# Recurrent gated attention and a gated MLP on one core: the written-out order of 944 operations, kept up to entry 385 and rewritten, with its engines, from there on

## Chip, core and metric

The kernel runs on one core of a Trainium2 chip. The metric is the device time of one execution in microseconds (us), the median of several runs; lower is better.

## What is computed

A recurrent attention over 768 steps (4 batches, 8 heads of 48) feeds a gated MLP block. The reference, cut:

```python
for t in range(S):                                      # B, H, S, D = 4, 8, 768, 48
    state = alpha[:, :, t, :, None] * state + einsum('bhd,bhe->bhde', k[:, :, t], v[:, :, t])
    y[:, :, t] = einsum('bhd,bhde->bhe', q[:, :, t], state)
x = y.transpose(0, 2, 1, 3).reshape(B, S, H * D)        # [4, 768, 384]
h = maximum(x @ w_in, 0)                                # d_ff = 1024
u, v = h[..., :512], h[..., 512:]
v_n = (v - mean(v)) / sqrt(var(v) + 1e-6)
v_s = einsum('ts,bsd->btd', w_spatial, v_n) + b_spatial[None, :, None]
return (u * v_s) @ w_out                                # [4, 768, 384]
```

## The kernel before, in words

The sequence of each batch is cut into six chunks of 128 steps; chunk n is chunk n mod 6 of batch n // 6, so there are 24. Within a chunk the recurrence becomes matrix products: running sums of log alpha (`cums`, function `single`, line 870), their exponentials (`einvs`, `eexps`, `ebc`), scaled k and q (`kts`, `qts`), their transposes for two chunks at once (`trk`, function `two_singles`, line 974; the two copies out of PSUM are `evs`), the scores (`sc`) and their masking (`ms`), the state's update (`upd`, then `z`, `S`, `sb` in `carry`, line 382) and the output (`y`), whose copy out is `xe`. Chunks 10 to 23, with which the change has to do, all go through `single` and `two_singles`; the earlier ones go in pairs and fours.

The MLP follows per batch b: `v.b.tt` and its relu `ve`, statistics `bn`, `rs`, `nm` and normalization `vn` (`project_v`, line 1054); `u.b.ft.th` and its relu `ue` (`project_u`, line 1103); the product with w_spatial `s.b.d.th` in two parts, the bias `se` and the gate `g` (`mix`, line 1122); the output product `o.b.tt`, its copy `oe.n` (n = 6b + tt) and its store `st.n` (`project_out`, line 1159). The u, v, s and o products all go through one helper, so line 1005 stands for all of them in the profile; likewise 178, 180, 184, 186 and 189 are helper lines for copies, relus and multiplications on any engine.

Each operation is made once as an object with a number, the engines it may run on, its dependencies and the PSUM banks that it takes. Nothing decides their order at run time. The table `PLAN` (line 42) lists all 944 in order, and `replay` (line 109) emits them as listed: the letter is the engine (P TensorE, D VectorE, A ScalarE, G GpSimd, S the SyncE queue that issues DMAs), the number is the operation, and what follows @ is its PSUM bank. An engine works its entries strictly in the order of the table; an entry waits for its dependencies and, when it takes a bank, for all readers of what the bank held before. There are eight banks. All loads and stores are issued by the one queue S; the loads of chunks 8 to 23 (q, k, v, alpha: `qcs`, `kcs`, `vcs`, `acs`) are 192 KB each in rows of 192 bytes, into rings of three slots for two chunks each. The last four output tiles are staged in the buffer of the first four, so that copies `oe.20` to `oe.23` wait for the stores `st.0` to `st.3`.

Numbers that are used below:

| table number | operation |
|---|---|
| 498, 564 | `lns`, log of alpha, chunks 12 and 15 (on A) |
| 499, 511, 565 | `cums`, running sums, chunks 12, 13 and 15 (on P) |
| 413 | `upd`, update of the state, chunk 10 (on P) |
| 374, 378, 372 | `u.1.1.0`, `u.1.3.0`, `u.1.0.0` (on P); their relus are 375, 379, 373 |
| 369, 380 | `v.1.2`, `v.1.3` (on P); their relus are 370, 381 |
| 419, 424 | `y`, chunks 10 and 11 (on P); their copies are 420, 425 |
| 266, 269, 272 | `o.0.3`, `o.0.4`, `o.0.5` (on P) |
| 368, 385 | `vn.1.1`, `vn.1.2` |
| 742, 748 | `trk`, transposes of chunks 18 and 19; `sc.18`, the scores that need both its copies, 743 and 744; 797 is one of the copies of the next pair |
| 452 | `s.1.2.0.0`, the first `s` of batch 1 in the new order |
| 701, 747, 756, 795, 846 | copy `oe.12` and casts `sb.18`, `sb.19`, `vbs.21`, `vbs.22` |
| 671, 691, 915 | `g.2.0.0`, `g.2.1.1`, `g.3.1.1`, gates; 907, 911 are `g.3.3.0`, `g.3.0.1` |
| 850, 857, 863, 872 | chunk 23: load of v, its cast `vbs`, the state's `S` of chunk 22, `y.23` |
| 704, 705 | `oe.13` and its store; 493, 265 and 259 are the stores `st.11`, `st.2` and `st.0` |
| 942 | `oe.23.1`, the last copy out of PSUM |

Of the kernel before, what the change touches and what calls it, by code (L numbers as in the profile page):

```python
# [57 lines left out]
D255 P348@7,6 D243 D327 D350 A393 P344@4 A394 P338@5 G31 G328 D397 D330 D349 G396 P404@3 A345 A339 A405 A406 P257@1  # L58
A395 S495 S390 A258 P260@4 P359@2 S402 G407 G248 G326 G329 S494 S560 P346@0,7 D408 P354@3,5 P410@1,6 A360 D331 A347
A353 A411 D356 D355 P362@2 G252 G398 P351@7 A352 P357@3 D412 S508 S497 S509 P421@6,1 P416@5,0 D361 S496 S507 S562 S550  # L60
S548 S611 S561 S551 S549 A358 A363 D418 D423 P511@7 P369@3 P413@0 P374@2 P380@1 D414 D417 A261 A512 P378@0 D422 A498
D364 A375 A564 P263@5 P499@6 G244 G332 G409 G256 A370 A379 A513 D371 G415 A500 A501 P419@0 P424@3 A425 G517 G505 G503
D381 D382 D516 G515 A420 P266@2 P269@4 A502 A365 A383 A270 D366 D504 P429@0 P426@1 P438@3 P440@6 D384 A368 A430 A427
P436@4 A437 A441 A385 D264 D439 P272@0 D367 D267 D428 D431 D386 P521@1 P372@4 A514 A273 P565@6 P376@2 A377 A432 A552
P442@7 A568 P529@0 D443 D522 P456@3 D433 D434 A435 A566 A567 D373 P452@7 P553@1 P518@2,5 A519 A554 A556 D520 A555 P457
D458 D530 D570 G569 G523 G557 G459 P444@4 P445 P448@5 D446 P453 D454 P468@6 P449 D558 D450 P533@7,4 P524@2,0 P572@1,3
D525 G451 G455 P472@5 P469 P460@2 P473 D526 D534 D535 G531 G447 D474 S623 A559 P575@7 D576 A573 P461 S625 S612 S563
A615 D470 D462 P616@4 P527@5 P536@1 A627 S613 A574 P579@7,3 P588@6,0 G577 A617 A528 D589 A618 A537 P628@5 A629 A571
G475 P538@2 A630 P464@1 S624 S614 S730 S718 S721 S626 S720 G620 D621 D581 D580 S733 S732 P476@6 G631 G578 P541@3
P584@7 A539 A619 A542 P465 S784 S719 A477 D632 P634@5,4 D590 A636 D466 D585 S731 A722 P591@3 S786 S772 S785 S773 S835  # L70
S774 A592 S787 S775 G622 G532 P582@1 A583 D635 D540 P637@7 P482@6 A633 A483 P723@5 G586 G471 D638 G639 A724 P645@3,4
P640@0,2 D543 G463 G587 P479@7 P604@6 P596@1 D646 D642 D641 A734 A726 D647 G729 G467 A605 A741 G727 P593@3 P600@6 A594
P735@0 D606 D595 A738 D480 P648@4 P643@3 A544 D545 D546 D597 A649 P488@2 A644 A788 A601 A489 D547 P653@4 P660@7 P745@6
A654 D746 D655 A736 A607 D608 D610 P491@3 P664@4 A661 A665 A737 P650@6 A492 A776 G739 P598@1 D651 D609 P485@4 D652
# [1190 lines left out]
```

## Time and profile before

| | |
|---|---|
| median of 3 runs | 138.32 us (138.22 to 139.34) |
| span of the profiled execution, first to last instruction | 137.9 us |
| granted TensorE clock | 1.000 |
| loads and stores by SyncE's queue | 28.32 MB |

The profile is of one execution. A time in a timeline is the start in us from the span's start, followed by the duration; equal instructions in a row are merged, and then the duration runs to the end of the last. A bracket at a line's end is the idle time of the engine before it and what ended it. A window's row gives the length of the stretch, then each engine's busy time with its instructions in brackets, the granted clock, the share of the 16 DMA engines and GB/s. The border between the kept entries and the others lies at about 54 us on TensorE; S works entries of the kept part until 62.65 us.

### The profile page before, as it was taken

The numbers are of one execution on the slowest core, as the hardware profiler recorded it, in microseconds if no ns is written. First come the engines' busy times: TensorE is split into PE (matmuls) and PEld (weight loads), VectorE is DVE, ScalarE is ACT, GpSimd is POOL, SyncE is SP. The second block draws the span as 40 slices with busy tenths as digits, with TensorE's granted clock in tenths as the row PEclk, the third lists the DMA queues.
The fourth block names the chain that finished last, engine by engine and source line by source line (L and its number), as shares of the span: only waits on it lengthen the run. The fifth ranks groups of instructions, "written<-read, shape, count | busy, mean of one in ns | idle before, by whom it ended". The sixth has DMA issues, their size and how long they took to land.

```text
span 137.9 us, 5298 instructions
## 1 busy us (share of the span) xinstructions
PE 130.1 (94%) x2108; PEld 79.4 (58%) x2122; DVE 120.2 (87%) x300; ACT 107.7 (78%) x261; POOL 86.6 (63%) x146
## 2 busy tenths in 40 slices
PE   6999998999999999799999999999999999999990
PEld 3365555565566556466657676656576765566560
DVE  6259999989989999899899999997999999974960
ACT  3476998999999799699997989999865796953040
POOL 7355899993499799761079989520799841004550
PEclk9999999999999999999999999999999999999999
DMA  3999999499989788699999898999960597101064
GB/s 88 370 372 381 344 349 361 106 373 382 355 162 281 159 168 165 124 186 188 193 204 201 164 209 156 189 186 216 213 134 5 187 349 270 63 0 57 0 233 172
DMA packets 76521, 28.66 MB, mean 208 GB/s; under 512 B 63056, under 2 KB 74960, under 8 KB 76496
## 3 DMA queue, kind: packets, MB, share of 16 engines
q1 hardware_dynamic: 76464, 28.32, 77.8%
q8 instruction: 16, 0.26, 0.8%
q14 instruction: 9, 0.07, 0.2%
q0 software_dynamic: 32, 0.00, 0.0%
HBM read 23.60 MB, written 4.72 MB: 205 GB/s over the span
## 4 chain that ended last, share of the span: by engine, by line
PE 60%; DMA 19%; POOL 8%; issue 3%; SPq 3%; ACT 3%; DVE 0%; POOLq 0%; ACTq 0%
PE bank L1005 43%; DMA raw_w<-in_moe_w_spatial_dram 6%; DMA kc<-in_k_dram 5%; DMA raw_w<-in_moe_w_out_dram 4%; DMA ac<-in_alpha_dram 4%; PE bank L960 3%; SPq L883 3%; PE bank L944 2%; PE bank L988 2%; PE bank L416 2%; POOL w_row L180 2%; POOL kt L189 2%; PE bank L932 1%; PE bank L898 1%; POOL state L189 1%
## 5 line engine op out<-in xcount | busy, mean ns | idle before, releaser
L1005 PE MATMUL bank<-w_spT,vn 128*128 128x384 bf16 x192 | 35.6, 327 | 0.0
L189 POOL TENSOR_TENSOR gT<-vs,uT 128x384 bf16<-128x384 f32 x28 | 25.7, 933 | 14.1 <-DVE vs L1152 14.1
L189 POOL TENSOR_TENSOR kt<-kc,binv 128x384 bf16<-128x384 f32 x22 | 20.2, 928 | 22.3 <-ACT binv L908 15.2
L1005 PEld LDWEIGHTS <-vn 128*128 128x128 bf16 x192 | 17.5, 98 | 11.2 <-issue 0.3
L1005 PE MATMUL bank<-w_in,xT 128*128 128x512 bf16 x58 | 17.4, 380 | 1.6 <-ACT xT L178 0.7
L1005 PE MATMUL bank<-xT,w_in 128*128 128x384 bf16 x96 | 18.7, 326 | 0.0
L1005 PE MATMUL bank<-w_out_sb,gT 128*128 128x384 bf16 (+1 forms) x100 | 18.4, 320 | 0.0
L1152 DVE TENSOR_TENSOR vs<-bank,bsp_bc 128x384 f32<-128x384 f32 x31 | 16.3, 549 | 2.4 <-PE bank L1005 2.3
L949 DVE TENSOR_TENSOR ptm<-bank,mask 128x512 bf16<-128x512 f32 x28 | 17.9, 682 | 0.5 <-PE bank L944 0.3
L178 ACT COPY kqT<-bank 128x512 bf16<-128x512 bf16 (+1 forms) x20 | 15.0, 793 | 3.1 <-PE bank L988 1.9
L1067 DVE BATCH_NORM_STATS2 stats<-v_sb 128x6 f32<-128x512 bf16 x24 | 16.4, 683 | 0.6 <-ACT v_sb L184 0.5
L184 ACT ACTIVATE v_sb<-bank 128x512 bf16<-128x512 f32 x20 | 11.7, 597 | 2.0 <-PE bank L1005 1.7
L184 ACT ACTIVATE uT<-bank 128x384 bf16<-128x384 f32 x27 | 12.4, 494 | 0.7 <-PE bank L1005 0.6
L1005 PEld LDWEIGHTS <-w_in 128*128 128x128 bf16 x96 | 9.0, 97 | 6.7 <-DVE ptm L949 0.3
L189 DVE TENSOR_TENSOR qt<-qc,bank 128x384 bf16<-128x384 f32 x24 | 12.6, 545 | 0.2 <-DMA qc<-in_q_dram 0.2
L1005 PEld LDWEIGHTS <-gT 128*128 128x128 bf16 x100 | 9.2, 98 | 5.8
L178 ACT CAST xT<-bank 128x384 bf16<-128x384 f32 x23 | 10.4, 482 | 1.1 <-PE bank L416 0.8
L843 DVE TENSOR_TENSOR ptm<-bank,mask 128x512 bf16<-128x512 f32 x16 | 10.3, 683 | 0.2 <-PE bank L836 0.2
L242 PE MATMUL bank<-junk 128*128 128x512 f32 (+3 forms) x14 | 8.8, 763 | 1.0 <-DVE junk L1231 1.0
L1005 PEld LDWEIGHTS <-xT 128*128 128x128 bf16 x72 | 6.2, 97 | 6.2 <-ACT xT L178 1.2
L178 ACT COPY raw_w<-bank 128x384 f32<-128x384 f32 x8 | 3.8, 479 | 7.3 <-PE bank L1005 7.2
L393 DVE TENSOR_TENSOR zs<-bank,state 128x384 f32<-128x384 f32 x16 | 8.8, 548 | 0.5 <-PE bank L932 0.4
(162 smaller groups left out, 264.3 us busy)
## 6 DMA issues: line engine op xcount, KB each, us to landing
ac<-in_alpha_dram SPq DMA_DIRECT2D x14, 192.0 KB, 4.4
kc<-in_k_dram SPq DMA_DIRECT2D x14, 192.0 KB, 4.4
qc<-in_q_dram SPq DMA_DIRECT2D x14, 192.0 KB, 4.4
vc<-in_v_dram SPq DMA_DIRECT2D x14, 192.0 KB, 4.2
raw_w<-in_moe_w_spatial_dram SPq DMA_DIRECT2D x3, 768.0 KB, 7.8
out_dram<-raw_w SPq DMA_DIRECT2D x11, 192.0 KB, 2.1
out_dram<-o_sb SPq DMA_DIRECT2D x9, 192.0 KB, 2.0
ac<-in_alpha_dram SPq DMA_DIRECT2D x2, 768.0 KB, 6.7
```

The source lines that it names most:

```text
L178: nc.scalar.copy(out=out, in_=in_)
L184: nc.scalar.activation(out=out, in_=in_, func=AF.Relu)
L189: ENG[eng].tensor_tensor(out=out, in0=in0, in1=in1, op=ALU.mult)
L242: nc.tensor.matmul(out=banks[n][:, 0:cols].rearrange("p (a b) -> p a b", a=4), lhsT=junk, rhs=junk[:, None, 0:cols // 4].to_broadcast([128 ...
L393: lambda _: nc.vector.tensor_tensor(out=zs[i % 3], in0=tp(), in1=state[(i - 1) % 3], op=ALU.add),
L843: nc.vector.tensor_tensor(out=ptm[n2][:, ci, s], in0=banks[sl.bank].rearrange("p (hp t) -> p hp t", hp=HP), in1=mask[:, 3][:, None, :].to_ ...
L883: nc.sync.dma_start(out=t[x].rearrange("p hp s d -> p (hp s) d"), in_=src[b, :, c * C:c * C + C, :].rearrange("h s d -> s h d"))
L949: nc.vector.tensor_tensor(out=ptm[n2][:, ci, s], in0=banks[sl_p[s].bank].rearrange("p (hp t) -> p hp t", hp=HP), in1=mask[:, 2][:, None, : ...
L960: nc.tensor.matmul(out=place(to, 3 * hp + (0, 1, 1, 2)[x]), lhsT=heads(vb, hp, x), rhs=ptm[n2][:, ci, x // 2, hp, :], start=(turn == 0), s ...
L1005: nc.tensor.matmul(out=ps, lhsT=lhsT, rhs=rhs, start=first and n == 0, stop=last and n == len(pairs) - 1)
L1067: nc.vector.bn_stats(out=stats[tt % 2], in_=v_sb[n2][:, tt, :])
L1152: nc.vector.tensor_tensor(out=vs[d], in0=banks[sl.bank][:, 0:TH], in1=bsp_bc[:, th, :], op=ALU.add)
```

## The change

The table's first 385 entries stay word for word; the other 559 are the same operations with the same dependencies in another order. 46 of them change engine: among others `vn` four from A to D and four from D to A, `oe` five from D to A and two from A to D, `ue` three from D to A and two from A to D, `evs` three from D to A and two from A to D, `g` three from G to D and two from D to G, `vbs` three from A to G and three from G to A. By number of entries D goes from 140 to 133, A from 138 to 145, G stays at 55, P at 166 and S at 60. Of the 142 entries of P that take a bank, 128 take another one. No line of code outside the table changes.

The diff, cut to the lines that matter below:

```diff
@@ -58,33 +58,33 @@
 D255 P348@7,6 D243 D327 D350 A393 P344@4 A394 P338@5 G31 G328 D397 D330 D349 G396 P404@3 A345 A339 A405 A406 P257@1
 A395 S495 S390 A258 P260@4 P359@2 S402 G407 G248 G326 G329 S494 S560 P346@0,7 D408 P354@3,5 P410@1,6 A360 D331 A347
 A353 A411 D356 D355 P362@2 G252 G398 P351@7 A352 P357@3 D412 S508 S497 S509 P421@6,1 P416@5,0 D361 S496 S507 S562 S550
-S548 S611 S561 S551 S549 A358 A363 D418 D423 P511@7 P369@3 P413@0 P374@2 P380@1 D414 D417 A261 A512 P378@0 D422 A498
-D364 A375 A564 P263@5 P499@6 G244 G332 G409 G256 A370 A379 A513 D371 G415 A500 A501 P419@0 P424@3 A425 G517 G505 G503
-D381 D382 D516 G515 A420 P266@2 P269@4 A502 A365 A383 A270 D366 D504 P429@0 P426@1 P438@3 P440@6 D384 A368 A430 A427
-P436@4 A437 A441 A385 D264 D439 P272@0 D367 D267 D428 D431 D386 P521@1 P372@4 A514 A273 P565@6 P376@2 A377 A432 A552
...
-P668@0 D794 D755 D678 D782 G781 G795 D682 P799@7 P669 G793 D800 P689 G675 D690 D670 P742@6,4 P796@7,3 A851 A780 D797
-P696@5 A743 A798 G683 G679 P808@0 P697 P852@7 P840@6 A841 A842 A853 A843 A854 D744 P748@3,4 P757@1,2 D698 G801 G671
-D749 D809 D758 P692@5 P693 D694 D750 P684@3 P703@0 P685 P700@5 G846 D759 A701 D686 P706@4 D856 D845 D707 A704 P760@5
-A761 P751@0 A752 A802 P803@6,7 D805 G844 G855 P812@3,2 P858@4,5 G810 G687 G699 G691 A859 G695 D813 P762@0 S850 P861@7
...
-D871 D767 D870 D865 P828@7 A829 D830 P824@1 P820@3 P817@7 A821 A768 A818 A825 G863 P872@4 A873 S705 A716 S481 S259
-S268 S487 S265 S493 S490 S271 S708 S262 S478 S274 G811 P867@5 D819 P826@3 P822@1 D868 P877@4 D769 D771 A827 S717 A831
...
-P912@0 P913 P920@3 D906 D895 D918 G919 D907 P929@6 P923@2 P921 S711 A930 S931 A924 S925 S714 D914 D910 D911 P926@6
-G915 D922 P932@2 A933 D927 S928 S934 P938@3 D939 S940 P935@6 A936 S937 P941@3 D942 S943
+S548 S611 S549 A358 A261 G256 A363 P378@7 P511@4 D423 D417 P413@3 D414 D364 A498 P374@1 P369@5 P380@3 P499@2 G332 A512
+A379 A513 D418 D422 G244 P272@7 A370 D371 A365 A381 A375 A502 S561 S718 S551 S623 S613 A273 D366 D382 P372@0 P269@3
+A564 G409 P419@1 G415 P424@7 A373 D270 D420 A514 P565@6 P266@0 D516 D368 A425 S625 P429@7 P426@4 A566 A568 A383 A500
+P263@1 P440@3 D384 D385 D386 D367 A430 D431 A501 P376@7 S612 P436@5 S624 A427 D428 S563 A264 A267 A377 G505 G503
+P521@0 A567 A432 D522 A552 P452@1 P448@7 P456@0 S626 S614 S772 S784 D433 D570 A437 A441 P553@6 A556 A554 A555 G515
...
+P602@4 P688@1 P680@2 A791 A603 D657 D658 D659 S271 S848 P742@4,7 A778 A779 G793 S837 G781 D794 P677 D678 D754 G755
+D782 G679 P672@5 A744 P673 D674 P668@7 P669 D670 P681 A839 A743 P748@5,4 P796@0,6 P757@7,3 A797 A783 D682 A798 D749
...
+P852@3 A795 P808@6 P700@4 A853 D686 D690 D800 G801 A854 D694 A747 D701 D809 G855 A846 A842 P703@1 P706@7 P660@4 A704
+S836 G844 S849 P760@6 A761 P751@1 S705 A752 A661 A802 D707 D845 D856 P812@7,2 D814 D813 P803@0,5 D804 D805 S493 S265
+S850 P858@3,6 A859 A860 P765@1 P861@2 P762@7 P815@3 A816 P806@5 A807 S268 S702 P869@6,0 G810 D862 P864@2,4 P828@3 A763
...
+S478 A825 S490 S487 G903 D918 P890@4 P912@1 P913 S708 A891 D910 G907 P920@4 P929@3 P921 G911 G919 A930 S931 P923@2
+A924 S925 P926@3 A927 S928 D914 D915 D922 P932@4 P938@2 D939 A933 S934 S940 P935@3 A936 S937 P941@4 A942 S943
 """
```

More of the change, by code (lines that the diff above doesn't have):

```diff
@@ L65 @@
[L65 to L74, printed above, removed]
@@ L75 @@
-A486 A725 D747 P666@7 A667 D740 P602@6 P662@4 P789@3 A656 A603 P676@7 P672@0 P753@6 A599 A790 A791 P777@1 A778 A792
-A779 S484 S847 S836 S837 A839 A783 S838 S848 A663 S849 D657 D658 D659 D754 D728 P677 P673 P680@6 P688@5 D674 P681
-P668@0 D794 D755 D678 D782 G781 G795 D682 P799@7 P669 G793 D800 P689 G675 D690 D670 P742@6,4 P796@7,3 A851 A780 D797
-P696@5 A743 A798 G683 G679 P808@0 P697 P852@7 P840@6 A841 A842 A853 A843 A854 D744 P748@3,4 P757@1,2 D698 G801 G671
-D749 D809 D758 P692@5 P693 D694 D750 P684@3 P703@0 P685 P700@5 G846 D759 A701 D686 P706@4 D856 D845 D707 A704 P760@5
@@ L80 @@
-A761 P751@0 A752 A802 P803@6,7 D805 G844 G855 P812@3,2 P858@4,5 G810 G687 G699 G691 A859 G695 D813 P762@0 S850 P861@7
-P765@3 D814 D804 P712@2 P815@6 A756 A763 P806@0 A860 D862 D764 D857 A816 A807 A766 P864@5,7 P869@4,1 S702 P715@6 D866
-D871 D767 D870 D865 P828@7 A829 D830 P824@1 P820@3 P817@7 A821 A768 A818 A825 G863 P872@4 A873 S705 A716 S481 S259
-S268 S487 S265 S493 S490 S271 S708 S262 S478 S274 G811 P867@5 D819 P826@3 P822@1 D868 P877@4 D769 D771 A827 S717 A831
-A823 A878 A770 A713 D832 P874@3 D833 D834 P890@5 P888@1 P884@4 D879 D875 D876 A880 D881 D882 P916@6 P709@2 A710 P896@3
@@ L85 @@
-P886@7 P900@0 A887 A889 A885 A891 P892@2 D883 P897 D898 G899 P893 P901 P908@5 P909 D894 D902 P904@2 P905 G903 P917
-P912@0 P913 P920@3 D906 D895 D918 G919 D907 P929@6 P923@2 P921 S711 A930 S931 A924 S925 S714 D914 D910 D911 P926@6
-G915 D922 P932@2 A933 D927 S928 S934 P938@3 D939 S940 P935@6 A936 S937 P941@3 D942 S943
+S548 S611 S549 A358 A261 G256 A363 P378@7 P511@4 D423 D417 P413@3 D414 D364 A498 P374@1 P369@5 P380@3 P499@2 G332 A512
+A379 A513 D418 D422 G244 P272@7 A370 D371 A365 A381 A375 A502 S561 S718 S551 S623 S613 A273 D366 D382 P372@0 P269@3
@@ new lines @@
+A564 G409 P419@1 G415 P424@7 A373 D270 D420 A514 P565@6 P266@0 D516 D368 A425 S625 P429@7 P426@4 A566 A568 A383 A500
+P263@1 P440@3 D384 D385 D386 D367 A430 D431 A501 P376@7 S612 P436@5 S624 A427 D428 S563 A264 A267 A377 G505 G503
+P521@0 A567 A432 D522 A552 P452@1 P448@7 P456@0 S626 S614 S772 S784 D433 D570 A437 A441 P553@6 A556 A554 A555 G515
+P438@3 G517 P529@5 D435 D434 P453 D504 P518@2,4 S730 D530 D454 D519 P449 D450 A615 A439 D558 P444@1 P457 D458 P445
+D446 A520 P616@4 P442@6 A722 A443 P524@0,7 P533@2,3 S719 G557 A617 S721 D525 D535 G455 G569 S773 P572@1,5 A574 S731
@@ new lines @@
+D534 A619 S733 S720 S786 D526 A618 D621 P472@6 P468@0 P723@2 A724 A725 G559 P575@5 P473 P469 G531 S732 D573 D576
+P460@7 P464@1 A627 P628@5 P465 P461 A629 A630 G447 G459 D474 A523 D470 G451 P476@0 A477 P527@6 A528 D466 D462 D632
+P536@7 A537 G620 P579@1,4 D580 D581 P588@5,0 D589 G631 P634@6,3 A636 G571 P584@7 G577 P479@1 P541@4 A622 G578 A542
+G463 A532 A480 D585 D635 G586 D590 P538@5 A539 P637@7 P482@3 A483 P582@6 S785 D633 D540 D638 S835 P591@1 P640@5,0
+P645@3,4 D641 A583 A726 P593@6 S774 D647 A592 P604@7 D543 D642 D646 A788 G467 A734 A594 G475 A605 S847 G471 P491@5
@@ new lines @@
+A492 P596@6 P735@7 P488@4 S838 A776 P777@0 A544 A736 A489 G587 P643@5 D545 G727 G639 A737 A644 P648@3 A649 D606 D595
+D547 G729 P745@4 P598@1 A599 A607 A780 D597 D746 D608 D609 D610 P600@5 P653@3 P650@1 A601 A738 A654 A546 D651 P664@5
+P666@4 P485@3 A665 A486 D655 S775 S787 D652 P662@1 P789@5 A667 A792 A663 G739 A790 D740 D728 A656 G741 P753@6 P676@3
+P602@4 P688@1 P680@2 A791 A603 D657 D658 D659 S271 S848 P742@4,7 A778 A779 G793 S837 G781 D794 P677 D678 D754 G755
+D782 G679 P672@5 A744 P673 D674 P668@7 P669 D670 P681 A839 A743 P748@5,4 P796@0,6 P757@7,3 A797 A783 D682 A798 D749
@@ new lines @@
+D671 D750 D758 G675 P696@2 P697 G683 D698 G699 P840@0 P689 A841 A843 A851 D759 G756 P684@5 P685 P692@7 P799@2 P693
+P852@3 A795 P808@6 P700@4 A853 D686 D690 D800 G801 A854 D694 A747 D701 D809 G855 A846 A842 P703@1 P706@7 P660@4 A704
+S836 G844 S849 P760@6 A761 P751@1 S705 A752 A661 A802 D707 D845 D856 P812@7,2 D814 D813 P803@0,5 D804 D805 S493 S265
+S850 P858@3,6 A859 A860 P765@1 P861@2 P762@7 P815@3 A816 P806@5 A807 S268 S702 P869@6,0 G810 D862 P864@2,4 P828@3 A763
+D691 D871 P817@0 P824@7 P826@5 G811 G687 S262 A766 A829 A818 P820@0 D865 D870 D866 P867@4 A868 G695 G857 G863 P872@6
@@ new lines @@
+A873 P822@3 P874@4 D819 D830 P877@6 P888@2 A831 A823 D764 D832 A834 D833 A889 D767 A768 D875 P709@3 P712@1 A878 D769
+A771 A713 P884@4 A885 S714 S274 S481 A827 D876 D770 D879 A880 D881 D882 P715@6 P886@2 P904@1 P900@5 D821 A710 S711
+A883 P892@4 P896@3 P901 D887 P897 P905 P893 P916@2 P917 A716 S717 S259 D902 S484 D898 G899 P908@3 P909 D894 D895 D906
+S478 A825 S490 S487 G903 D918 P890@4 P912@1 P913 S708 A891 D910 G907 P920@4 P929@3 P921 G911 G919 A930 S931 P923@2
+A924 S925 P926@3 A927 S928 D914 D915 D922 P932@4 P938@2 D939 A933 S934 S940 P935@3 A936 S937 P941@4 A942 S943
```

## The prediction

> **What bounds the kernel now.** I read the page first, then the stretches of the part that changes, then the chain, the waits and the timeline of single engines.
>
> ```profile
> PE 130.1 (94%) x2108; PEld 79.4 (58%) x2122; DVE 120.2 (87%) x300; ACT 107.7 (78%) x261; POOL 86.6 (63%) x146
> ```
>
> ```profile
> 54.00:60.00 6.00, 4.91 (x91) 3.19 (x89) 5.36 (x12) 4.80 (x13) 4.18 (x8) 1.00 0.76 150
> 60.00:70.00 10.00, 9.95 (x101) 6.20 (x101) 9.07 (x25) 9.57 (x28) 2.83 (x4) 1.00 0.99 193
> ...
> 90.00:100.00 10.00, 9.96 (x76) 5.95 (x75) 9.07 (x25) 9.45 (x28) 3.71 (x5) 1.00 1.02 210
> 100.00:110.00 10.00, 9.84 (x217) 6.83 (x217) 9.79 (x19) 6.63 (x16) 9.36 (x12) 1.00 0.38 100
> ...
> 120.00:134.00 14.00, 14.00 (x90) 8.39 (x89) 10.18 (x23) 4.96 (x12) 5.26 (x20) 1.00 0.17 61
> ```
>
> TensorE is the bound. The change begins at about 54 us, and from 60 to 134 us TensorE rests for hardly 0.1 us in ten. Only the first stretch has a hole: 1.09 us of 6. A busy share could still hide matmuls that stand in line, so the chain, which gives counts, comes next.
>
> ```profile
> 51.62 5.70 DMA ac<-in_alpha_dram
> ...
> 58.42 0.39 ACT uT L184
> ...
> 118.39 10.67 PE bank L1005 x63
> ```
>
> ```profile
> L1005 PE MATMUL bank<-w_spT,vn 128*128 128x384 bf16 x144 | 26.4, 327 | 0.0
> L1005 PE MATMUL bank<-w_in,xT 128*128 128x512 bf16 x40 | 11.7, 379 | 0.5 <-ACT sbd L178 0.2
> ```
>
> ```profile
> PE bank L960 <- ACT uT L184: 1.0, 1, 1.0
> ```
>
> 63 products of 384 columns in 10.67 us are 0.169 us each, though one is shown as 0.327 long: they overlap, and that spacing is TensorE's pace. The work itself isn't changed, so a new order can win only the time in which TensorE waits. In the whole part that changes the view of waits knows one such wait of size, 1.0 us at line 960. The timelines say where it comes from:
>
> ```profile
> 53.18 0.87 ACT L178 CAST xT<-bank 128x384 bf16<-128x384 f32 x2
> ...
> 57.41 0.52 ACT L888 ACTIVATE la<-ac 128x384 bf16<-128x384 f32 x1 [1.09 <-DMA ac<-in_alpha_dram]
> 57.84 0.58 ACT L184 ACTIVATE v_sb<-bank 128x512 bf16<-128x512 f32 x1
> 58.32 0.48 ACT L184 ACTIVATE uT<-bank 128x384 bf16<-128x384 f32 x1
> 58.69 0.49 ACT L910 ACTIVATE bank<-bank 128x384 f32<-128x384 f32 x1
> 59.09 0.49 ACT L908 ACTIVATE binv<-bank 128x384 bf16<-128x384 f32 x1
> ```
>
> ```profile
> 57.41 0.33 PE L898 MATMUL bank<-la,le_one 128*128 128x384 bf16 x1
> 57.58 0.24 PE L901 MATMUL bank<-ones_col,la 128*128 128x1 bf16 x4
> 58.85 0.41 PE L960 MATMUL bank<-ptm,vb 128*32 128x128 bf16 x16 [1.03 <-ACT uT L184]
> ...
> 59.24 0.41 PE L960 MATMUL bank<-ptm,vb 128*32 128x128 bf16 x16
> ```
>
> ScalarE's A564 (log of alpha, chunk 15) stood 1.09 us for a load that landed at 57.33 (51.62 + 5.70). The relu A379 is queued behind it, P419 (`y.10`) needs the bank that A379 reads, and TensorE stood 1.03 us.
>
> **The change, part by part.**
>
> *A564 goes back in ScalarE's queue.* It was the 7th of ScalarE's entries after the border; now it is the 14th, behind A379 and six more. From the rows at 58.32, 58.69 and 59.09 a step of ScalarE is about 0.39 us, 0.48 behind a 512-wide relu; 0.42 is my mean. The second of the two copies at 53.18 is the first entry behind the border and begins at about 53.6, so A564 comes at 53.6 + 13 x 0.42 = 59.1, well behind the landing at 57.33, whose load is in the kept part. The wait of 1.09 is gone, and with it 1.03 on TensorE: the gain.
>
> *What is late next.* P565 (`cums.15`) needs A564, and it has been moved forward too. Ahead of it TensorE now has three `u` (9 x 0.169 = 1.52), two `v` (six of 512 columns; 0.052 longer each by the two means above, so 6 x 0.22 = 1.32), two `o` (8 x 0.169 = 1.35), two `cums` (0.3 to 0.4 each, rows 57.41 and 57.58), one `upd` of four quarter-wide products (0.17) and two `y` (0.39 from 58.85 to 59.24, and 0.5): 5.9. It is reached at 54.0 + 5.9 = 59.9, and A564 ends at 59.1 + 0.5 = 59.6. Slack 0.3 with the mean step; with 0.48 for each step it ends at 60.3 and TensorE loses 0.4. Bounds 0 and 0.6 (the copy A425 follows it closely for `v.1.5`); I take 0.2.
>
> *Engines.* VectorE gives up seven entries net and ScalarE gets seven, some 4 us of each at 0.5 to 0.6. The exchange is uneven in a useful way:
>
> ```profile
> L178 ACT COPY kqT<-bank 128x1024 bf16<-128x1024 bf16 x8 | 8.0, 1013 | 2.0 <-PE bank L988 1.9
> ...
> L1096 DVE TENSOR_SCALAR vn<-v_sb,mvs,rstd 128x512 bf16<-128x512 bf16 x14 | 5.4, 403 | 0.0
> ...
> L1092 ACT ACTIVATE vn<-v_sb,shift,rstd 128x512 bf16<-128x512 bf16 x4 | 3.3, 818 | 0.2 <-DVE shift L1084 0.2
> ```
>
> In batch 1 three `vn` leave ScalarE (3 x 0.82) for VectorE (3 x 0.40), and relus and copies of nearly one price on both go the other way. ScalarE, at 9.57 of 10 there, is relieved by about half a us; nothing is lost. But the first `s` of batch 1, P452, is now TensorE's 22nd entry behind the border where the first was the 25th, three `u` (1.5 us) earlier, and needs all four `vn.1.0` to `vn.1.3` in a chain of statistics, `rs`, `nm`, `vn`. Bounds 0 and 1.0; I take 0.2, since the four on VectorE are now 0.4 each and adjoining.
>
> In batch 2 it is the opposite: ScalarE receives `vn.2.0` (0.82), two of the wide copies A744 and A797 (1.0 each) and three casts (A747, A795, A846, 0.5 each), and gives up a cast and a copy (756, 701; 0.5 each): 3.3 us between 90 and 110, where the windows leave it 0.55 + 3.37 = 3.9. It fits, but late. The spot is P748 (`sc.18`): P742, the transposes, is now TensorE's 90th entry instead of the 99th, and before `sc.18` both copies must be out, both on ScalarE.
>
> ```profile
> 101.18 1.93 ACT L178 COPY kqT<-bank 128x1024 bf16<-128x1024 bf16 x2 [0.88 <-PE bank L988]
> ...
> 101.69 1.27 DVE L180 COPY kqT<-bank 128x1024 bf16<-128x1024 bf16 x2
> ```
>
> Between P742 and P748 TensorE has two first and four second parts of `s`: 16 x 0.169 = 2.7 us. ScalarE has copy, log, copy: 0.97 + 0.4 + 0.97 = 2.3, after two exponentials (0.8) that can lie beside P742's own half us. Cover 3.2 against 3.1. Bounds 0 and 1.0; I take 0.2.
>
> *Gates on VectorE.* 671, 691 and 915 go there, 907 and 911 leave.
>
> ```profile
> 128.28 0.55 DVE L189 TENSOR_TENSOR gT<-vs,uT 128x384 bf16<-128x384 f32 x1
> ...
> 129.44 1.97 POOL L189 TENSOR_TENSOR gT<-vs,uT 128x384 bf16<-128x384 f32 x2 [1.68 <-DVE vs L1152]
> ...
> 130.72 1.09 DVE L189 TENSOR_TENSOR gT<-vs,uT 128x384 bf16<-128x384 f32 x1
> ```
>
> The same gate took 0.55 while GpSimd was idle and 1.09 while GpSimd ran its own, so a moved gate costs VectorE 0.55 to 1.09. 671 falls among GpSimd's gates of batch 2: 0.5 at worst, on an engine that has 0.9 us free in 90 to 100; 15 entries of TensorE lie between the product that it gates and `o.2.0`, which reads it. I put it at nothing; without that cover it would be 0.5. The Trainium skill, "SBUF — State Buffer", section "Who interferes with whom", says that a VectorE instruction with two inputs in SBUF contends with a GpSimd instruction that reads SBUF; the doubled row agrees, and by it alone the move speaks against this change. By it the sum would be up to 0.5 higher if one of the three gates were on the path, and as it stands otherwise.
>
> *Loads.* The order of S changes from its 40th entry on, but the loads are the same, and the engines that carry them are full to about 100 us (DMA share 0.99 and 1.02 above), so each position keeps its time. The one that moves in time is the last, S850 (v of chunk 23), now behind the stores S705, S493 and S265.
>
> ```profile
> 100.31 0.63 SPq L883 DMA_DIRECT2D vc<-in_v_dram  x1
> 107.72 0.83 SPq L1184 DMA_DIRECT2D out_dram<-o_sb  x2
> ```
>
> ```profile
> vc<-in_v_dram SPq DMA_DIRECT2D x14, 192.0 KB, 4.2
> ...
> out_dram<-raw_w SPq DMA_DIRECT2D x11, 192.0 KB, 2.1
> ```
>
> ```profile
> 116.30 0.41 PE L960 MATMUL bank<-ptm,vb 128*32 128x128 bf16 x16
> ```
>
> ```profile
> L189 POOL TENSOR_TENSOR state<-zs,bc 128x384 f32<-128x384 f32 x5 | 4.2, 836 | 0.7 <-DVE zs L393 0.7
> ...
> L180 POOL CAST vb<-vc 128x384 bf16<-128x384 f32 x8 | 4.0, 505 | 1.8 <-DMA vc<-in_v_dram 1.8
> ```
>
> S705 waits for A704, the copy of `o.2.1`; before, its store was the second of the two at 107.72, so A704 had ended by 108.1, and with the gain it ends at about 107.7. Three issues of 0.42 (0.83 / 2) put S850 at 109.0 instead of 100.31; it lands at 113.2, or 114.7 with the 5.70 of the load above. Behind it on GpSimd wait G857 (0.5) and G863 (0.84), and P872 (`y.23`) waits for both: ready at 114.6 or 116.1. P872 is the 133rd entry of TensorE in both orders and ran at 116.30, so its turn is at about 115.9. Price nothing, or 0.2; I take nothing.
>
> *The end.* (Rows below.) A942 replaces D942 as the last copy, 192 columns. VectorE took 0.36, ScalarE 0.48 for 384 columns; below that for half of them, so between -0.1 and +0.1: nothing. S259 (`st.0`), for which the copy at 130.77 must wait, now stands behind the stores of `oe.15` to `oe.17`; ScalarE had done all its earlier work 5.56 us before that copy, at 125.2, so `st.0` is out at 125.7 and has landed, with 2.1, by 127.8: three us of cover, nothing; without them each us late would be one at the end.
>
> ```profile
> 130.77 0.48 ACT L178 COPY raw_w<-bank 128x384 f32<-128x384 f32 x1 [5.56 <-PE bank L1005]
> ...
> 134.02 0.48 ACT L178 COPY raw_w<-bank 128x384 f32<-128x384 f32 x1 [0.50 <-PE bank L1005]
> 134.35 0.36 DVE L180 COPY raw_w<-bank 128x192 f32<-128x192 f32 x1 [0.62 <-PE bank L1005]
> ```
>
> **The sum.** Span 137.9 - 1.03 + 0.2 + 0.2 + 0.2 = 137.5. The runs' median, 138.32, lies 0.4 above this span, and I keep that distance: 137.9 us.
>
> **The rivals.**
>
> *All is kept.* The new order gives nothing back and other small rests go too: 138.32 - 1.03 = 137.3, down to 136.8 if the half us of rests between 60 and 134 went as well (0.05 + 0.04 + 0.16 in the three ten-us stretches shown, about as much in the others). For it: VectorE, at 9.1 to 9.8 of 10 before, has 4 us less to do. Against: three places with 0.1 to 0.3 us of slack.
>
> *The wait only changes its name.* TensorE stands for A564 at P565 instead of for A379 at P419, or for the `vn` of batch 1, about 1 us: 138.3.
>
> *ScalarE becomes the bound at 90 to 103 us.* It had 0.55 us free in 90 to 100 and gets 1.8 (`vn.2.0` and one wide copy) before P748 is due. If its lateness is passed on whole, P748 starts 1.3 late and the next pair of copies, both on ScalarE again, adds its excess over VectorE, 0.97 - 0.64 = 0.3 each: 137.9 + 1.9 = 139.8.
>
> *The last load is too late.* It decides as soon as S850 lands after about 114.5 (115.9 less 0.5 and 0.84). If the landing takes 5.7 us and has the bytes of one of the three stores in front (2.1 by the row of stores), it is at 109.0 + 7.8 = 116.8, `y.23` is ready at 118.2, 2.3 after its turn, and behind it in TensorE's queue stands all the rest: 137.9 + 2.3 = 140.2, slower. Against it: before, the engines of the DMA were at 0.38 in this stretch.
>
> **How the numbers follow.** Forecast 0.50; all is kept 0.20, of which 0.12 below 136.94; the wait changes its name 0.12; ScalarE 0.10; the last load 0.08. About 1% (1.4 us) is what a measurement of this kernel can tell from no change. Faster by more: 0.12; slower by more: 0.10 + 0.08, and 0.04 out of the forecast for small losses at many of the 166 entries together: 0.22; within 1%: 0.66. The range goes from 136.8, all kept, to 139.9, between the two slow rivals. The likeliest case alone: 137.3 to 138.5.
>
> **What would show it.** Right: ScalarE's 1.09 us wait for alpha's load and TensorE's 1.03 us are gone; VectorE's busy time falls by about 4 us, ScalarE's rises by as much; from 60 us on TensorE still shows 9.8 or more of 10; S850 is issued after 107 us and GpSimd's cast behind it shows a DMA wait, but line 960 has none. Wrong: a TensorE wait of over 0.5 us at line 898 or 960 near 60, at 1005 near 65, at 944 near 99, or at 960 near 115; each names its step. A shift of the span without any such wait would mean that the products' spacing depends on their order, which I have put at nothing.

## The result: slower, 139.87 us against 138.72

| | before | after |
|---|---|---|
| median | 138.72 us (138.12 to 139.34, 7 runs) | 139.87 us (139.45 to 140.5, 7 runs) |
| profiled execution | span 137.9 us | span 138.3 us, 140.12 us in all |

The ratio is 1.0086, 95% interval 1.0059 to 1.0113: about 1.2 us slower (0.0086 x 138.7), where the forecast was 0.4 faster. The ratios of this study leave out the few executions that took over 1.5% longer than the fastest of their kernel, two of them 440 and 707 us; the medians are of all. The time of an execution is 1.73 to 1.85 us more than its span in every run of this study, so the profiled execution of before, with its span of 137.9, took about 139.7 us (an estimate: its own time isn't on record), 1.4 more than the 138.32 from which the forecast started. That difference turns out to matter.

The busy times of the page of after, and the stretches of the view of windows (PE, PEld, DVE, ACT, POOL busy, then the clock and the DMA share):

```profile
PE 129.7 (94%) x2108; PEld 78.5 (57%) x2122; DVE 119.0 (86%) x293; ACT 110.9 (80%) x268; POOL 87.5 (63%) x146
```

```profile
54.00:60.00 6.00, 5.95 (x106) 3.73 (x101) 5.86 (x16) 5.93 (x17) 4.61 (x8) 1.00 0.96 186
60.00:70.00 10.00, 9.28 (x103) 5.26 (x93) 9.11 (x23) 8.84 (x28) 3.27 (x4) 1.00 1.03 203
...
90.00:100.00 10.00, 9.95 (x94) 5.90 (x93) 8.81 (x25) 9.83 (x28) 2.74 (x4) 1.00 0.77 161
```

The hole has moved. Before, TensorE was busy 4.91 of 6 in the first of these and 9.95 of 10 in the second; now it is 5.95 and 9.28. Its waits, by the view of waits after 54 us, and its entries in the timeline:

```profile
PE bank L1005 <- DVE state L189: 0.4, 1, 0.4
PE bank L1005 <- ACT bc L915: 0.2, 1, 0.2
PE bank L1005 <- ACT xT L178: 0.2, 1, 0.2
PE bank L932 <- ACT raw_w L178: 0.2, 1, 0.2
```

```profile
62.94 1.63 PE L1005 MATMUL bank<-xT,w_in 128*128 128x384 bf16 x9
64.72 0.33 PE L932 MATMUL bank<-vb,kt 128*128 128x96 bf16 x4 [0.16 <-ACT raw_w L178]
64.89 1.46 PE L1005 MATMUL bank<-w_spT,vn 128*128 128x384 bf16 x8
66.76 0.81 PE L1005 MATMUL bank<-w_spT,vn 128*128 128x384 bf16 x4 [0.41 <-DVE state L189]
67.67 0.34 PE L898 MATMUL bank<-la,le_one 128*128 128x384 bf16 x1
```

Only the first and the last row of the view of waits lie between 62 and 70 us, 0.6 us together; the other two stand at 85.14 and 113.04. That view doesn't list every rest, so I read the spacing as well. Products of 384 columns that nothing holds up start 0.163 us apart (nine of them take from 61.73 to 63.20 in the second profile of before). By that, `upd.12` at 64.72 is 0.31 late (62.94 and nine spacings are 64.41), `s.1.3.0.0` at 66.76 another 0.57 and `cums.14` at 67.67 another 0.26: 1.1 us in all. The second profile of before loses hardly 0.1 between 62 and 70 us.

The whole new part can be compared in the same way, because its products are the same in every order. It goes from the start of the last kept product on TensorE to the end of TensorE's last product:

```profile
53.77 0.62 PE L944 MATMUL bank<-kqT 48*128 48x128 bf16 x16
...
131.08 3.42 PE L1005 MATMUL bank<-w_out_sb,gT 128*128 128x384 bf16 x24
```

That is 80.73 us in after (53.77 to 134.50), and 80.73 to 80.74 in three profiles of it.

`upd.12` waits for ScalarE's copy of `o.0.3` (`oe.3`). The reason for the other two stands in VectorE's and GpSimd's timelines of after:

```profile
61.26 0.41 DVE L1096 TENSOR_SCALAR vn<-v_sb,mvs,rstd 128x512 bf16<-128x512 bf16 x1
...
66.15 0.56 DVE L189 TENSOR_TENSOR state<-bank,bc 128x384 f32<-128x384 f32 x1
...
67.07 0.55 DVE L189 TENSOR_TENSOR qt<-qc,bank 128x384 bf16<-128x384 f32 x1
```

Three more `vn` follow from 62.32 to 64.61, 2.29 us in all. One at a time, and with the two multiplications of GpSimd beside them:

```profile
62.32 0.40 DVE L1096 TENSOR_SCALAR vn<-v_sb,mvs,rstd 128x512 bf16<-128x512 bf16 x1
62.64 1.05 DVE L1096 TENSOR_SCALAR vn<-v_sb,mvs,rstd 128x512 bf16<-128x512 bf16 x1
63.61 1.00 DVE L1096 TENSOR_SCALAR vn<-v_sb,mvs,rstd 128x512 bf16<-128x512 bf16 x1
```

```profile
62.63 0.91 POOL L189 TENSOR_TENSOR kt<-kc,binv 128x384 bf16<-128x384 f32 x1 [4.02 <-ACT binv L908]
63.50 0.96 POOL L189 TENSOR_TENSOR kt<-kc,binv 128x384 bf16<-128x384 f32 x1
```

The `vn` at 61.26 takes 0.41 while GpSimd rests, and the one at 62.32, which began 0.31 ahead of GpSimd's multiplications for chunks 12 and 13 (`kts.12` and `kts.13`, table numbers 503 and 515), takes 0.40. The other two began 0.01 and 0.11 behind such a multiplication; they take 1.05 and 1.00, and each ends 0.15 after it (63.69 against 63.54, 64.61 against 64.46). So the price is no fixed slowing: a `vn` stands for what is left of the multiplication that began first. (A later one, at 96.62, began with 0.29 of a multiplication left; it takes 0.44, and again ends 0.15 after it.) What stands behind the three on VectorE is 1.1 us late: S.12, whose read frees the bank of `s.1.3.0.0`, and the `qt` of chunk 15 (`qts.15`, number 570), which frees the bank that `cums.14` needs. The Trainium skill, "SBUF — State Buffer", section "Who interferes with whom", states that `tensor_scalar` in its two-port modes contends with GpSimd, and that the one that issues first blocks the other wholly. The contention and the order agree with these rows, though no row shows the mode. That the block is whole is not shown: a `vn` needs 0.40 alone, and each of the two ended 0.15 behind the multiplication. GpSimd paid 0.05 at most (0.96 against 0.91).

### The profile page after: what moved, and what is told of

It is laid out like the page before. It is cut to its first block, busy times and chain, and to the rows that moved or that the text cites. A ratio compares the mean times of both kernels' runs of the same rounds, so it can differ in the third digit from the quotient of the medians.

```text
span 138.3 us, 5293 instructions
## 1 busy us (share of the span) xinstructions
PE 129.7 (94%) x2108; PEld 78.5 (57%) x2122; DVE 119.0 (86%) x293; ACT 110.9 (80%) x268; POOL 87.5 (63%) x146
## 4 chain that ended last, share of the span: by engine, by line
PE 60%; DVE 14%; ACT 11%; DMA 5%; issue 4%; POOL 2%; SPq 0%; ACTq 0%; POOLq 0%; DVEq 0%
PE bank L1005 42%; DMA kc<-in_k_dram 5%; DVE ptm L949 3%; DVE stats L1067 3%; DVE vn L1096 3%; ACT xT L178 3%; PE bank L854 2%; ACT kqT L178 2%; PE bank L988 2%; ACT uT L184 2%; PE bank L898 2%; PE bank L416 2%; PE bank L836 2%; PE bank L960 1%; PE bank L944 1%
## 5 line engine op out<-in xcount | busy, mean ns | idle before, releaser
L1005 PE MATMUL bank<-xT,w_in 128*128 128x384 bf16 x96 | 19.2, 326 | 0.0
L178 ACT COPY kqT<-bank 128x512 bf16<-128x512 bf16 (+1 forms) x21 | 16.0, 805 | 3.0 <-PE bank L988 1.9
L1005 PE MATMUL bank<-w_in,xT 128*128 128x512 bf16 x58 | 16.2, 380 | 1.7 <-ACT xT L178 0.9
L184 ACT ACTIVATE uT<-bank 128x384 bf16<-128x384 f32 x28 | 13.3, 493 | 4.2 <-PE bank L1005 4.2
L242 PE MATMUL bank<-junk 128*128 128x512 f32 (+3 forms) x14 | 7.9, 689 | 1.1 <-DVE junk L1231 1.1
L1096 DVE TENSOR_SCALAR vn<-v_sb,mvs,rstd 128x512 bf16<-128x512 bf16 x18 | 8.5, 497 | 0.0
```

Of the source, the lines that this page charges most:

```text
L178: nc.scalar.copy(out=out, in_=in_)
L184: nc.scalar.activation(out=out, in_=in_, func=AF.Relu)
L242: nc.tensor.matmul(out=banks[n][:, 0:cols].rearrange("p (a b) -> p a b", a=4), lhsT=junk, rhs=junk[:, None, 0:cols // 4].to_broadcast([128 ...
L1005: nc.tensor.matmul(out=ps, lhsT=lhsT, rhs=rhs, start=first and n == 0, stop=last and n == len(pairs) - 1)
L1096: nc.vector.tensor_scalar(out=vn[n2][:, x, :], in0=v_sb[n2][:, x, :], scalar1=mvs[n2][:, x, 0:1], scalar2=rstd[n2][:, x:x + 1], op0=ALU.su ...
```

## The experiments

All times are set against runs of before beside them on the same chip. The theories: M, the mechanism of my forecast (the wait for alpha was worth 1 us, and something gave more back); R, the wait belonged to one execution and there was nothing to win; C, VectorE held up by GpSimd; Q, the order of TensorE's and ScalarE's own entries costs the time; T and E, part of the loss lies in the tail, behind the last product.

### Before, once more

No edit.

> The kernel before, once more, so that its span, its time and its waits are seen in another execution. Theory M (a real gain, given back): ScalarE's wait for alpha of chunk 15 and TensorE's wait behind it are again near 1 us; ratio 1.000. Theory R (the wait was a chance of the one execution that was profiled): the wait is under 0.5 us, the span is near 136.9, and the time lies about 1.8 us above the span, as it does for the changed kernel; ratio 1.000 as well.

138.56 us (12 runs), ratio 1.0016 [0.9991, 1.0040]; span 137.2. ScalarE's timeline, TensorE's, and the two ends of the new part:

```profile
56.70 0.52 ACT L888 ACTIVATE la<-ac 128x384 bf16<-128x384 f32 x1
```

```profile
57.90 0.33 PE L898 MATMUL bank<-la,le_one 128*128 128x384 bf16 x1
...
58.23 0.41 PE L960 MATMUL bank<-ptm,vb 128*32 128x128 bf16 x16
```

```profile
53.96 0.62 PE L944 MATMUL bank<-kqT 48*128 48x128 bf16 x16
...
130.93 2.77 PE L1005 MATMUL bank<-w_out_sb,gT 128*128 128x384 bf16 x20
```

The log of alpha has no wait, nor has `y.10` at 58.23, and the new part takes 79.74 us (53.96 to 133.70), 1.0 less than in after. In the first profile of before it took 80.83 (53.48 to 134.31), the 1.03 of the wait more. The kernel before with another end, below, is a third profile of this order: 79.73, and no such wait either. Alpha of chunk 15 landed at 57.33 in the first profile and at 54.70 in each of the other two. SyncE's queue shows it too, the first row from the first profile, the second from this one:

```profile
53.22 3.78 SPq L883 DMA_DIRECT2D vc<-in_v_dram  x2
```

```profile
53.24 1.95 SPq L883 DMA_DIRECT2D vc<-in_v_dram  x2
```

The same two issues took 1.83 us longer there, and this once the loads were later than the order's cover. The spans say how usual that is: the 82 further executions of before that were timed with the experiments and count in their ratios lie between 136.3 and 137.7, so that the profiled 137.9 lies above them all. R is shown: the wait is no usual part of the time that the runs measure. A span alone wouldn't show it, for the border itself, behind work that all these kernels share, comes between 53.05 and 54.17 us in the profiles.

### The new order with before's engines

Each new entry has the letter that the operation had before (`A420` for `D420`, `D373` for `A373` and so on).

> The new table with every entry's engine as before: order, banks and queue S are new, the 46 changes of engine are undone. If the engines (VectorE's normalizations that run beside GpSimd's multiplications above all) cost the time, the ratio falls from 1.0086 to 1.000 or below, and VectorE's wait for its normalizations near 62 us is gone. If the order itself costs it, VectorE has about 4 us more to do than in the changed kernel and the ratio is 1.010 or more.

161.16 us (6 runs), ratio 1.1616 [1.1562, 1.1671]. Neither size expected. From the view of waits after 54 us:

```profile
POOL gT L189 <- DVE vs L1152: 26.7, 8, 14.9
...
PE bank L932 <- ACT vb L178: 5.2, 3, 2.2
```

GpSimd stood 14.9 us at one gate for VectorE's spatial bias, TensorE 5.2 us in all for ScalarE's casts of v (line 178). The order is made for its engines and can't be judged without them; this says nothing on where the 1.2 us are.

### Before with the log of alpha moved back

```diff
-A564 P263@5 P499@6 ... A420
+P263@5 P499@6 ... A420 A564
```

> The kernel before with one entry moved: ScalarE's logarithm of alpha of chunk 15 (564) stands behind the copy 420 instead of seven entries earlier. Theory M: TensorE's 1.03 us wait near 58 us is gone and nothing else changes, 1.0 us less, ratio 0.993. Theory R: the wait is seldom that long, ratio 0.998 to 1.001.

139.56 us (9 runs), ratio 1.0068 [1.0038, 1.0099]. The step on which my gain rested, done alone in the old order, gains nothing and costs 0.9 us, which R hadn't expected either. M falls. TensorE's new part takes 80.14 us (54.08 to 134.22), 0.4 more than in before; 0.29 of it stand at `o.0.5`, which starts at 63.61 where 63.32 was due. Where the other 0.5 lies is open.

### After with before's order of loads

The S entries of the new part in the order of before, all else as in after.

> The new table with the loads and stores in the order of before (queue S alone undone; the load of v of chunk 23 is ahead of the stores again). If the queue's order costs the time, the ratio falls from 1.0086 to 1.002 or less. If not, it stays at 1.006 to 1.011, since the loads of the new order come in time.

147.13 us (6 runs), ratio 1.0591 [1.0545, 1.0637]. The same view:

```profile
ACT la L888 <- DMA ac<-in_alpha_dram: 6.1, 1, 6.1
...
PE bank L1005 <- ACT uT L184: 4.8, 1, 4.8
```

ScalarE's log stood 6.1 us for one load of alpha, and TensorE 4.8 for a relu queued behind it. The new order of S belongs to the table too. This run can't tell whether that order costs anything by itself; but after's own trace shows no wait of ScalarE or TensorE for a load behind the border, so nothing in it points to the queue.

### After with kts.13 and kts.12 earlier

The two are put ahead of `vbs.12`; `einvs.12` (500) and `ebc.12` (502) change places on ScalarE, so that the input of `kts.12` is there in time.

```diff
-... A375 A502 ... G415 ... A383 A500 ... G505 G503 ... G515
+... A375 A500 ... G415 G515 G503 ... A383 A502 ... G505 ...
```

> The kernel after, with GpSimd's two multiplications kts.13 and kts.12 put ahead of the cast vbs.12 and the reciprocal-exponential einvs.12 that they wait for put in the place of ebc.12 on ScalarE (the two change places, both about 0.4 us), so that GpSimd does them at about 59 to 61 us and is idle while VectorE runs the three vn that began at 62.32. Nothing else is moved; the arithmetic is the same. Theory C (the loss is VectorE held up by GpSimd): the three vn take about 1.2 us instead of 2.29, the state sum S.12 starts near 65.2 instead of 66.15, TensorE's rests between 62 and 70 us fall by 0.7 to 1.1 us of 1.3, and the ratio to before is 1.001 to 1.004 instead of 1.0086. Rival Q (the loss comes from the order of TensorE's and ScalarE's own entries in 62 to 70 us): the vn may get shorter, but the ratio stays at 1.007 to 1.010. Rival T (the loss is in the tail and in many small places): the rests of 62 to 70 us go, and the ratio stays at 1.005 or more.

139.3 us (12 runs), ratio 1.0059 [1.0029, 1.0089]; after itself, beside it on the same chip, 1.0120. VectorE, GpSimd, TensorE's wait and the ends of the new part now:

```profile
62.34 1.16 DVE L1096 TENSOR_SCALAR vn<-v_sb,mvs,rstd 128x512 bf16<-128x512 bf16 x3
...
65.30 0.56 DVE L189 TENSOR_TENSOR state<-bank,bc 128x384 f32<-128x384 f32 x1 [0.19 <-PE bank L932]
```

```profile
59.95 1.78 POOL L189 TENSOR_TENSOR kt<-kc,binv 128x384 bf16<-128x384 f32 x2 [1.75 <-DMA kc<-in_k_dram]
```

```profile
PE bank L932 <- ACT raw_w L178: 0.2, 1, 0.2
```

```profile
53.80 0.62 PE L944 MATMUL bank<-kqT 48*128 48x128 bf16 x16
...
130.77 2.94 PE L1005 MATMUL bank<-w_out_sb,gT 128*128 128x384 bf16 x21
```

The three vn take 1.16 instead of 2.29, S.12 starts 0.85 earlier, the waits at `s.1.3.0.0` and `cums.14` are gone, and the median falls by 0.9 us against after. The new part takes 79.91 us (53.80 to 133.71): 0.82 of after's 1.0 are gone. C is shown with its size, and Q falls. The exchange of the two exponentials was not tried alone; that the gain comes by way of VectorE is read from these rows. The `vn` at 61.28 now pays instead, 0.61, and it too ends 0.15 after the multiplication beside it (61.89 against 61.74), but nothing that TensorE needs is made late by it.

Yet T, the rests gone and 1.005 or more left, fits as well: the ratio is above my 1.001 to 1.004, and 0.8 us were left. TensorE has little of it, 0.17 of its new part (79.91 against 79.74). But from the last copy's end to the end of the span it is 3.57 us, where before has 3.15. More of the loss that is left sits behind the last product than ahead of it.

### After with S.12 ahead of the statistics, and both edits

```diff
-D428 ... D522
+D522 D428
```

> The kernel after, with one entry of VectorE moved: the statistics of v.1.4 (0.68 and 0.18 us) go behind the state sum S.12 instead of ahead of it. The three vn stay beside GpSimd at 2.29 us. Theory C, in the narrower form that TensorE stands for S.12 (its bank is the one that s.1.3.0.0 needs): S.12 starts 0.8 us earlier, the wait of 0.41 at s.1.3.0.0 goes, but rs.1.4 and with it vn.1.4 and vn.1.5 come 0.5 us later; ratio 1.003 to 1.007. If the lateness of VectorE as a whole is the cause, whatever stands in its queue: 1.007 to 1.010, with the wait at another product.

> The kernel after with both edits: kts.13 and kts.12 earlier on GpSimd, and the statistics of v.1.4 behind S.12 on VectorE. Theory C: as the first alone or up to 0.3 us better, ratio 0.999 to 1.004, S.12 starts near 64.8. Rival Q: 1.007 to 1.010.

140.19 us, ratio 1.0127 [1.0088, 1.0167], and 140.08, 1.0122 [1.0085, 1.0159] (6 runs each). Both miss their ratios: I had taken S.12 to be what TensorE stands for. S.12 did start as early as expected, at 65.29 and 64.72, and the wait at `s.1.3.0.0` is gone; TensorE stands at another product. The waits of the first and of the second:

```profile
PE bank L898 <- DVE qt L189: 1.2, 1, 1.2
```

```profile
PE bank L898 <- DVE qt L189: 1.0, 1, 1.0
```

GpSimd and VectorE in the second:

```profile
60.44 1.83 POOL L189 TENSOR_TENSOR kt<-kc,binv 128x384 bf16<-128x384 f32 x2 [2.83 <-DMA kc<-in_k_dram]
```

```profile
61.75 1.69 DVE L1096 TENSOR_SCALAR vn<-v_sb,mvs,rstd 128x512 bf16<-128x512 bf16 x3
...
64.72 0.56 DVE L189 TENSOR_TENSOR state<-bank,bc 128x384 f32<-128x384 f32 x1 [0.46 <-PE bank L932]
...
66.69 0.34 DVE L1084 TENSOR_SCALAR shift<-mvs,rstd 128x1 f32<-128x1 f32 x2 [0.60 <-ACT rstd L1078]
```

The wait only goes on to `cums.14`: `qts.15` is queued behind `shift`, which needs `rstd` from ScalarE, which needs the statistics that I had put back. In the second kernel the load of k came later, so that the kts ran beside the vn again and three of these took 1.69; S.12 is early all the same, and the lateness of `shift` eats what that gives. So S.12 is not the one entry that TensorE stands for: VectorE's queue as a whole is late, and of the two orders tried the one with the statistics first is the better.

### After, once more

No edit.

> The kernel after, unchanged, on the same chip as the other three, so that they can be set against it: ratio 1.006 to 1.011 again, and the same rests of TensorE between 62 and 70 us, with vn at 0.73 us each beside GpSimd's kt, if they belong to the order and not to one execution. If they were chance as the wait for alpha was in the first profile of before, the three vn take 1.2 us here and the ratio still is near 1.009.

140.2 us (6 runs), ratio 1.0120 [1.0077, 1.0163], just above what was expected, with the vn again at 2.29 for three (0.41, 1.05 and 1.00, not 0.73 each) and the same lateness at the same three products. Unlike the wait for alpha it belongs to the order.

### The end: four empty memsets more, and four less

Behind its last entry GpSimd has IDLE = 16 empty memsets (line 1233). From the last copy's end to the end of the span it is 3.15 or 3.16 us in the first three profiles of the old order and 3.42 in after, 3.57 in the kernel with the earlier kts. GpSimd's stream has 204 instructions in the trace of before, 200 in that of after and 201 with the earlier kts; its computations are the same, but 37, 33 and 34 separate waits go with them.

```diff
-IDLE = 16
+IDLE = 20      (after: 204 instructions)
+IDLE = 12      (before: 200 instructions)
```

> The kernel after with IDLE 20 instead of 16: four more of the empty memsets at the end of GpSimd's stream, nothing else. In the profiles the end from the last copy to the end of the span was 3.15 us in every execution of the old order and 3.42 in every one of the new, with a rest of 0.32 before GpSimd's clearing of the semaphores, and GpSimd's stream is 200 instructions there instead of 204 (33 waits instead of 37); the last 8 KB of instructions were fetched after the end of the span instead of 5 us before it. Theory E (GpSimd stands for its own instructions at the end, and where that stand falls depends on the count): with 204 again the rest is gone, copy to end is 3.15, the span is 0.3 shorter, ratio 1.006 to 1.010 where the kernel after had 1.0086 and 1.012. Rival (the rest belongs to the last copy being on ScalarE): 3.42 stays.

> The kernel before with IDLE 12 instead of 16: four empty memsets less on GpSimd, 200 instructions, and nothing else; the reverse of the first. Theory E: a rest of about 0.3 us before GpSimd clears the semaphores, copy to end 3.4 instead of 3.15, ratio 1.001 to 1.004 with the last copy still on VectorE. Rival (the rest belongs to the new order or to the last copy on ScalarE): 3.15 and 1.000 (0.998 to 1.002).

After with 20: 139.7 us (12 runs), 1.0088 [1.0059, 1.0117]; from copy to end 3.14. Before with 12: 138.96 us (12 runs), 1.0028 [1.0001, 1.0055]; 3.43. Both are as theory E had them. A ratio alone is too coarse for 0.3 us; the profiles are not. The following rows give SyncE's waits at the end and GpSimd's clearing of the semaphores, in after, in after with 20, in before and in before with 12 (name of the operation, count, shortest/median/longest ns, first and last start):

```profile
L1260 SPq EVENT_SEMAPHORE  x8: 17/28/28, 136.9 to 138.3; - x8
...
L1260 POOLq EVENT_SEMAPHORE_RANGE_CLEAR  x1: 139/139/139, 137.9 to 137.9; - x1
```

```profile
L1260 SPq EVENT_SEMAPHORE  x8: 17/28/28, 136.8 to 137.9; - x8
...
L1260 POOLq EVENT_SEMAPHORE_RANGE_CLEAR  x1: 142/142/142, 137.5 to 137.5; - x1
```

```profile
L1260 SPq EVENT_SEMAPHORE  x8: 17/28/28, 136.1 to 137.2; - x8
...
L1260 POOLq EVENT_SEMAPHORE_RANGE_CLEAR  x1: 142/142/142, 136.8 to 136.8; - x1
```

```profile
L1260 SPq EVENT_SEMAPHORE  x8: 17/28/28, 135.6 to 137.0; - x8
...
L1260 POOLq EVENT_SEMAPHORE_RANGE_CLEAR  x1: 139/139/139, 136.6 to 136.6; - x1
```

From the first of these waits to the clearing it is 1.0, 0.7, 0.7 and 1.0 us: with 200 instructions there is a rest of 0.3 ahead of the clearing, with 204 none, in either order and whichever engine makes the last copy. That the end depends on the count is shown in both directions. What GpSimd stands for may be the loading of its own instructions. In the view of DMAs, cut to the stretch from 138 us on, after has its last load of 8 KB on queue 14:

```profile
q14 instruction: 1, 0.01, 2.5%
```

In the kernels with 204 the last such load comes at 131 to 133 us, while GpSimd runs its empty memsets and nobody waits for it. The Trainium skill, "Runtime: NRT & Kernel Launch", section "Instruction fetch mechanics", calls the crossing from one block of instructions to the next mostly hidden. If the rest is such a crossing, it cost 0.3 us here. That is argued from the place and the count, not shown; and since after's load comes at 138.6, behind the clearing at 137.9, the rest was not a wait for these 8 KB.

### Both causes removed

The kernel with the earlier kts and IDLE = 19 (204 instructions); then the same with the copy `oe.3`, for whose bank `upd.12` waits, moved up on ScalarE:

```diff
-A430 ... A501 ... A427 ... A264 A267
+A430 A267 ... A501 ... A427 ... A264
```

> The kernel after with kts.13 and kts.12 earlier on GpSimd (the first edit before, ratio 1.0059 then, 201 instructions, copy to end 3.57) and IDLE 19, which makes GpSimd's stream 204 again. If theories C and E are both right their terms add: 0.9 and 0.4 us less than the kernel after, ratio 1.001 to 1.004. If the end can't be shortened: 1.005 to 1.007.

> As the one before, and the copy of o.0.3 (oe.3), whose bank the product upd.12 needs, two relus and a bias earlier in ScalarE's queue (it moves ahead of the exponential and the relu of v.1.4). The rest of 0.39 at upd.12 goes, and it was the last one between 54 and 134 us that the kernel before has not: ratio 0.998 to 1.002, at best 0.2 us under the kernel before. Rival (something else of VectorE's or ScalarE's work is then late, as when S.12 was put first): no gain over the one before, or slower.

138.53 us (12 runs), ratio 1.0005 [0.9972, 1.0038], from copy to end 3.13; and 138.77 us (12 runs), 1.0031 [0.9999, 1.0064]. The first came out just under its 1.001 to 1.004: with C and E both gone, nothing is left of the loss that these runs can tell from none. The second missed its 0.998 to 1.002, as its rival had it: the edit took the rest at `upd.12` away and 0.26 came back at `cums.14`, and the new part takes 79.97 us instead of 79.92. No version beats the kernel before.

## Why the prediction was wrong

*"The wait of 1.09 is gone, and with it 1.03 on TensorE: the gain."* This step failed. The wait is gone, as ScalarE's timeline of after shows: the log starts at 59.21 (I had said 59.1) without a rest.

```profile
59.21 0.53 ACT L888 ACTIVATE la<-ac 128x384 bf16<-128x384 f32 x1
```

But I took 1.03 from the median of runs that did not have it. In the two profiles of before's order with the usual loads TensorE has no wait above 0.2 us between 54 and 134 us, and the whole gain is 0. The sign was there: I set the median against the span of 137.9 as if 0.4 lay around it, where 1.8 does.

*The first `s` of batch 1, 0.2, "since the four on VectorE are now 0.4 each and adjoining".* The step that made the loss, 0.82 us on TensorE in place of 0.2. The `vn` came in time for the products; what I mis-sized is their price beside GpSimd, 1.05 and 1.00 for two of them in place of 0.4, and I left out who is queued behind them. I had held the moved gates against GpSimd, and not asked which entry of GpSimd's new order stands beside the moved vn. The page's groups, before (second profile) and after:

```profile
L1096 DVE TENSOR_SCALAR vn<-v_sb,mvs,rstd 128x512 bf16<-128x512 bf16 x18 | 7.2, 419 | 0.0
```

```profile
L1096 DVE TENSOR_SCALAR vn<-v_sb,mvs,rstd 128x512 bf16<-128x512 bf16 x18 | 8.5, 497 | 0.0
```

These 1.3 us are half of why VectorE's busy time fell by 1.4 us, from 120.4 in the second profile of before, and not by 4; ScalarE's rose by 3.2, near the 4 forecast.

*P565 against A564, 0.2, and P748, 0.2.* TensorE shows no wait at either; both were nothing. The row of 90 to 100 us has ScalarE at 9.83 of 10, so that it was close, as forecast.

*Gates at nothing.* Held: no wait of TensorE behind them.

*Loads and the last load.* Held. SyncE and GpSimd:

```profile
109.54 0.41 SPq L883 DMA_DIRECT2D vc<-in_v_dram  x1
```

```profile
112.70 0.50 POOL L180 CAST vb<-vc 128x384 bf16<-128x384 f32 x1 [0.88 <-DMA vc<-in_v_dram]
```

The issue came at 109.5 (forecast 109.0), the cast waited for it at 112.70 (forecast 113.2), and `y.23` did not wait.

*The end.* The last copy on ScalarE costs nothing: with 204 instructions copy to end is 3.14 there, 3.15 with VectorE. The 0.3 behind it was in no term, since I looked at the last entries and not at the length of GpSimd's stream.

*The sum with measured terms.* TensorE's new part grows by 0.99 (80.73 less 79.74), of which 0.82 go with the earlier kts (80.73 less 79.91), and 0.27 are at the end (3.42 less 3.15): 1.26, against 1.2 [0.8, 1.6] by the ratio. That 139.87 still falls into the range of 136.8 to 139.9 is luck: its upper end came from ScalarE and the last load, and neither cost anything. The "wrong" sign "at 1005 near 65" named the right place (0.57 us by the spacing, 0.41 by the view of waits); the rival nearest to it, the wait that changes its name at the `vn` of batch 1, had the place and the price of about 1, and ended at 138.3 only because the same wait was counted as gained.

## What to carry to other kernels

Before a wait is counted as a gain, see whether the profiled execution is a usual one: compare its full time with the median, and look whether the wait hangs on a load that happened to be late. When an operation is moved to VectorE, its price is that beside what GpSimd does in the new order: look which of the two begins first there, and what is queued behind it on VectorE and will be late with it. To set two orders of the same work against each other, measure the bounding engine from one product that both share to its last: here that repeats within 0.02 us, while the spans differ by more than 1 us. A change that alters only the number of waits can lengthen the end of a kernel: 0.3 us here.

## What the runs showed of the hardware that was not expected

- A `vn` of 128 x 512 in bf16 on VectorE takes 0.38 to 0.41 us alone, or when it begins 0.31 ahead of a GpSimd multiplication; begun 0.01 and 0.11 behind one it takes 1.05 and 1.00 and ends 0.15 after it. GpSimd's 0.91 becomes 0.96 at most.
- The same order has executions whose loads are late for a while: one load landed at 57.33 us in one profile and at 54.70 in two others. The spans of that order go from 136.3 to 137.9 us.
- A rest of 0.3 us at the end comes and goes with four instructions of GpSimd, about 0.2% of the time.
